# Leaving out the all-zero quarter of a causal score block, with half of the heads' keys exchanged between partition halves

## Chip, cores and metric

One core of a Trainium2 chip. The metric is the device time of one execution in microseconds (us), the lower the better. Before the change it was 703.62 us, the median of 3 runs (702.62 to 704.25).

## The reference, cut to what matters

A retention layer (attention with a decay instead of a softmax) followed by a dense layer with a gated activation. Batch 4, 8 heads, 768 positions, head size 64; then 3072 tokens through 512 -> 2048 -> 512.

```python
def _attn_ref(q, k, v):
    ...
    for t in range(S):
        state = gamma[None, :, None, None] * state + np.einsum('bhd,bhe->bhde', k[:, :, t], v[:, :, t])
        y[:, :, t] = scale * np.einsum('bhd,bhde->bhe', q[:, :, t], state)
    return y

def _moe_ref(x, w_in, w_out):
    h = x @ w_in
    g = h * (1.0 / (1.0 + np.exp(-1.702 * h)))
    return g @ w_out
```

## The kernel before

All is fp32. The sequence is cut into 24 chunks of 128 positions. For a chunk the kernel computes the scores of its 128 queries against its own 128 keys, multiplies them with a mask that holds the decay and is zero where the key is later than the query, and takes the values with them; what lies before the chunk comes from a state of 64x64 per head. Chunks are woven into the dense layer's matmuls. From chunk 8 on (block 2 of four chunks) they are "late": they run between the down-projections, in a steady pattern.

The heads lie as pairs (r, s): r is the head's half of the partitions in the transposed q and k, s its place there. `i` below is r and `h` is the half of the keys.

```python
    def attend(j, f=None):          # scores of chunk j, and the rest of chunk f = j - 1
        if j is not None:
            p = ps_a.tile([P, 2, HP, P], F32, name="pa", tag="pa")
            kt, qt = KT.pop(j), QT[j]
            for hp in range(HP):
                for h in range(2):
                    for i in range(2):
                        r, t = slice(i * D, (i + 1) * D), slice(h * D, (h + 1) * D)
                        pe.matmul(p[t, i, hp, :], kt[r, hp, t], qt[r, hp, :], start=True, stop=True)
        if f is not None:
            finish(f)
        if j is not None:
            AT[j] = home(j, "at")
            for i in range(2):
                dve.tensor_mul(AT[j][:, i], p[:, i], mask[:, i])
            if j > 2 * CB:
                decay(j)            # GpSimd: keys times their decay, for the state
        ...

    def finish(j):
        ...
        if c:                       # what the state gives: 64 rows x 64 columns of the array
            for out, s, r in where:
                k = slice(r * D, (r + 1) * D)
                pe.matmul(out, old[k, s, :], qt[k, s, :], start=(s < 2), stop=False, ...)
        for out, s, r in where:     # values: 128 rows x 64 columns
            pe.matmul(out, vn[:, HP * r + s, :], a[:, r, s, :], ...)
        if c < NC - 1:              # update of the state: 128 rows x 64 columns, 64 moving columns
            ...
```

At the end of a block GpSimd also makes four sums of X, the input of the next block's up-projection (`sums_x`), which TensorE needs in its third group of products.

Of the kernel before, what the change touches and what calls it, by code (L numbers as in the profile page):

```python
# [9 lines left out]
F32 = mybir.dt.float32  # L10
U32 = mybir.dt.uint32
AF = mybir.ActivationFunctionType
ALU = mybir.AluOpType
P = 128
# [14 lines left out]
def kernel(  # L29
# [29 lines left out]
    pe, act, dve, pool, sp = nc.tensor, nc.scalar, nc.vector, nc.gpsimd, nc.sync  # L59
    ctx.enter_context(tc.manual_schedule(engines={mybir.EngineType.PE}))  # L60

    B, H, S, D = q.shape
    NT, DM = out.shape
    DFF = moe_w_in.shape[1]
    HP = H // 2
    NC = S // P
    NCH = B * NC
    CB = 4
# [9 lines left out]
    const = ctx.enter_context(tc.tile_pool(name="const", bufs=1))  # L78
    one = ctx.enter_context(tc.tile_pool(name="one", bufs=1))
    two = ctx.enter_context(tc.tile_pool(name="two", bufs=2))  # L80
    ps_a = ctx.enter_context(tc.tile_pool(name="ps_a", bufs=1, space=bass.MemoryType.PSUM))
# [13 lines left out]
    X1 = W2[:, 6].rearrange("p (s c) t -> p s c t", s=4)  # L95
    rowd = const.tile([P, HP, P], F32, name="rowd")
    cold = const.tile([P, 2 * H], F32, name="cold")
    whole = const.tile([P, 2, 2], F32, name="whole")
    ident = const.tile([P, P], F32, name="ident")
    mask = const.tile([P, 2, HP, P], F32, name="mask")  # L100
    state = [const.tile([P, HP, D], F32, name=f"state{i}") for i in range(2)]


    QKV = {}

    def load(j, what="qkv"):


        b, c = divmod(j, NC)
        rows = slice(c * P, (c + 1) * P)  # L110

        def plain(name, src, tag, bufs, pairs=False, engine=sp):
            t = two.tile([P, H, D], F32, name=name + "_in", tag=tag, bufs=bufs)
            QKV[name, j] = t
            src = src[b, :, rows, :].rearrange("h p d -> p h d")
            if pairs:
                for i in range(2):
                    engine.dma_start(t[:, i:H:2, :], src[:, i * HP:(i + 1) * HP, :])
            else:
                sp.dma_start(t, src)  # L120

        if j < 2 * CB:
            if "q" in what:
                plain("q", q, "q_sq", 2, True)
                plain("kn", k, "k_sq", 2, True, sp if j else act)
        elif "q" in what:
            for name, src in (("q", q), ("k", k)):
                t = two.tile([P, HP, P // C4, C4], F32, name=name + "_sq")
                for r0 in range(0, P, C4):
                    d0 = r0 % D  # L130
                    for hp in range(HP):
                        tc.keep_in_program_order(sp.dma_start(
                            t[r0:r0 + C4, hp],
                            src[b, hp + HP * (r0 // D), rows, d0:d0 + C4].rearrange("(s p) d -> p s d", p=C4)))
                QKV[name, j] = t
        if "v" in what:
            if j >= 2 * CB and c < NC - 1:
                plain("kn", k, "kn", 1)
            plain("v", v, "v", 2)
# [63 lines left out]
    QT, KT, KD, AT = {}, {}, {}, {}  # L203

    def home(j, name):

        at = ["qT", "kT", "kd", "at"].index(name)
        shape = [[HP, P], [HP, P], [H, D], [2, HP, P]][at]
        if j >= 2 * CB:
            return one.tile([P] + shape, F32, name=name, tag=name, bufs=2 - (at > 0))  # L210
        if at < 3:
            t = G[:, at, j % 2 * 2:j % 2 * 2 + 2]
            return t.rearrange("p s t -> p (s t)").rearrange("p (a b) -> p a b", a=shape[0])
        return G[:, 3 + j % 2].rearrange("p s t -> p (s t)").rearrange("p (a b c) -> p a b c", a=2, b=HP)
# [22 lines left out]
    def decay(j):  # L237

        if j % NC == NC - 1:
            return  # L240
        KD[j] = home(j, "kd")
        x = QKV.pop(("kn", j)).rearrange("p h d -> p (h d)")
        x = x.rearrange("p (s r d) -> p r s d", s=HP, r=2) if j < 2 * CB else x.rearrange("p (r s d) -> p r s d", r=2, s=HP)
        pool.tensor_mul(KD[j].rearrange("p (r s) d -> p r s d", r=2), x,  # L244
                        cold[:, H:2 * H].rearrange("p (r s) -> p r s", r=2)[:, :, :, None].to_broadcast([P, 2, HP, D]))

    def attend(j, f=None):


        if j is not None:  # L250
            p = ps_a.tile([P, 2, HP, P], F32, name="pa", tag="pa")
            kt, qt = KT.pop(j), QT[j]
            for hp in range(HP):
                for h in range(2):
                    for i in range(2):
                        r, t = slice(i * D, (i + 1) * D), slice(h * D, (h + 1) * D)
                        pe.matmul(p[t, i, hp, :], kt[r, hp, t], qt[r, hp, :], start=True, stop=True)  # L257
        if f is not None:
            finish(f)
        if j is not None:  # L260
            AT[j] = home(j, "at")
            for i in range(2):
                dve.tensor_mul(AT[j][:, i], p[:, i], mask[:, i])  # L263
            if j > 2 * CB:
                decay(j)
        if f is not None and f + 2 < 2 * CB:
            load(f + 2, "v")
        if j is not None and 2 * CB < j < NCH - 1:
            load(j + 1, "v")

    def finish(j):
        c = j % NC
        old, new = state[c % 2], state[(c + 1) % 2]
        vn, a, qt = QKV.pop(("v", j)), AT.pop(j), QT.pop(j)


        y = ps_a.tile([P, 2, HP, P], F32, name="py", tag="py")
        where = [(y[s % 2 * D:(s % 2 + 1) * D, r, s // 2, :], s, r) for s in range(HP) for r in range(2)]
        if c:
            for out, s, r in where:  # L280
                k = slice(r * D, (r + 1) * D)
                pe.matmul(out, old[k, s, :], qt[k, s, :], start=(s < 2), stop=False, skip_group_check=True)  # L282
        for out, s, r in where:
            pe.matmul(out, vn[:, HP * r + s, :], a[:, r, s, :], start=(not c and s < 2), stop=(s >= 2),  # L284
                      skip_group_check=True)
        if c < NC - 1:

            kd = KD.pop(j)
            u = y[:, 0, 2:4, :].rearrange("p o t -> p (o t)").rearrange("p (s d) -> p s d", s=HP)
            for s in range(HP):  # L290
                for r in range(2):
                    pe.matmul(u[r * D:(r + 1) * D, s, :], kd[:, HP * r + s, :], vn[:, HP * r + s, :],  # L292
                              start=False, stop=True, skip_group_check=True)
        half, t0 = divmod(j % CB * P, TH)
        x = X1 if j // CB == 1 else X
        dve.tensor_mul(x[:, 2 * half:2 * half + 2, :, t0:t0 + P], y[:, :, 0:2, :],
                       rowd.rearrange("p (r o) t -> p r o t", r=2))
        if c == 0:
            dve.tensor_copy(new, u)
        elif c < NC - 1:  # L300
            pool.tensor_mul(new, old, whole.rearrange("p a b -> p (a b)")[:, :, None].to_broadcast([P, HP, D]))
            dve.tensor_add(new, new, u)
# [168 lines left out]
    first = const.tile([P, 1], F32, name="first")  # L471
# [10 lines left out]
            pe.transpose(idle[:, 0, :], ident, ident)  # L482


    for i in range(2):
        for hp in range(HP):
            h = HP * i + hp
            dve.tensor_copy(mask[:, i, hp, :], cold[:, h:h + 1].to_broadcast([P, P]))
    m3 = mask.rearrange("s i h t -> s (i h) t")
    pool.affine_select(out=m3, in_=m3, compare_op=ALU.is_ge, fill=0.0, base=0,  # L490
                       pattern=[[0, H], [1, P]], channel_multiplier=-1)

    def chunks(first, last):

# [30 lines left out]
    between = chunks(CB + 1, 2 * CB - 1) + [lambda: attend(None, 2 * CB - 1)]  # L525
    for n, unit in enumerate([(1, p) for p in range(3)] + [(half, p) for p in range(3, NP) for half in range(2)]):
        up0(*unit, "xxyx"[n % 4])
        if n % 2 == 0:
            narrow()
        if n in (0, 2, 4, 6, 8, 9, 11):  # L530
            between.pop(0)()
    for f in range(NFF):
        up1(f)
        if f % 2 == 0:
            narrow()
        if f >= NFF - 4:
            sums_w2(2 * (f - NFF + 4))
        if f >= NFF - 2:
            load(2 * CB + f - NFF + 2, "qkv" if f == NFF - 2 else "qk")
    for m in range(NB):  # L540
        between = []
        if m == 0:
            between = [lambda: turn(2 * CB), lambda: attend(2 * CB), lambda: None, lambda: None, lambda: turn(2 * CB + 1)]
        elif m == 1:
            between = [lambda: (decay(2 * CB), load(2 * CB + 1, "v"))] + chunks(2 * CB + 1, 3 * CB)[1:]
        elif 1 < m < NB - 2:
            between = chunks((m + 1) * CB + 1, (m + 2) * CB)
        elif m == NB - 2:
            between = chunks((m + 1) * CB + 1, NCH - 1) + [lambda: attend(None, NCH - 1)]
# [59 lines left out]
```

## Time and profile before

| | before |
|---|---|
| time, median of 3 | 703.62 us |
| TensorE busy | 686.3 of 701.9 us |
| one late chunk, from its first record to the next full-array matmul | 3.01 us |
| of it scores / state / values / update | 0.93 / 0.54 / 0.93 / 0.61 us |
| first down-projection to the end of the program | 539.0 us |

A record is one matmul instruction in the trace. The rows of the chunk are read from start to start in TensorE's timeline, because the records' lengths overlap. The prediction below shows those lines.

### The profile page before, as it was taken

The numbers are of one execution on the slowest core, as the hardware profiler recorded it, in microseconds if no ns is written. First come the engines' busy times: TensorE is split into PE (matmuls) and PEld (weight loads), VectorE is DVE, ScalarE is ACT, GpSimd is POOL, SyncE is SP. The second block draws the span as 40 slices with busy tenths as digits, with TensorE's granted clock in tenths as the row PEclk, the third lists the DMA queues.
The fourth block names the chain that finished last, engine by engine and source line by source line (L and its number), as shares of the span: only waits on it lengthen the run. The fifth ranks groups of instructions, "written<-read, shape, count | busy, mean of one in ns | idle before, by whom it ended". The sixth has DMA issues, their size and how long they took to land.

```text
span 701.9 us, 11046 instructions
## 1 busy us (share of the span) xinstructions
PE 686.3 (98%) x4493; PEld 572.5 (82%) x4493; DVE 361.5 (52%) x521; ACT 125.8 (18%) x197; POOL 129.7 (18%) x126
## 2 busy tenths in 40 slices
PE   6799999999999999999999999999999999999997
PEld 5588885447888888888888888888888888888886
DVE  3989889993711822443742453453345362344241
ACT  3213333311000001331000332000333000233000
POOL 4221000000466404000324000132200143000030
PEclk9899999999999999999999999999999999999999
DMA  9884343421130224200334300324300210000001
GB/s 230 264 231 133 135 136 135 138 35 28 28 65 27 63 46 103 46 1 15 72 62 91 65 1 8 72 45 90 74 0 3 60 30 13 34 1 1 15 1 45
DMA packets 138754, 46.36 MB, mean 66 GB/s; under 512 B 130176, under 2 KB 131216, under 8 KB 138704
## 3 DMA queue, kind: packets, MB, share of 16 engines
q1 hardware_dynamic: 134704, 38.84, 23.2%
q0 software_dynamic: 1856, 5.52, 2.1%
q10 hardware_dynamic: 2144, 1.31, 0.6%
q8 instruction: 35, 0.57, 0.3%
q14 instruction: 15, 0.12, 0.1%
HBM read 39.33 MB, written 6.29 MB: 65 GB/s over the span
## 4 chain that ended last, share of the span: by engine, by line
PE 93%; DVE 5%; DMA 1%; ACT 0%; SPq 0%; issue 0%; ACTq 0%
PE pd L432 39%; PE px L381 16%; PE py L381 12%; PE ph L329 8%; PE ph L342 8%; PE py L284 4%; PE pa L257 3%; PE py L292 1%; PE py L282 1%; DMA q_in<-in_q_dram 1%; DVE W L371 1%; DVE G L371 1%; PE pt L225 1%; DVE G L372 1%; DVE W L372 1%; DVE W L198 0%
## 5 line engine op out<-in xcount | busy, mean ns | idle before, releaser
L432 PE MATMUL pd<-W,G 128*128 128x256 f32 x1120 | 247.4, 381 | 0.4 <-DVE G L372 0.3
L432 PEld LDWEIGHTS pd<-W,G 128*128 128x128 f32 x1120 | 211.4, 190 | 30.4 <-DVE G L372 1.2
L381 PE MATMUL px<-X,W 128*128 128x256 f32 x512 | 119.0, 379 | 0.0
L381 PEld LDWEIGHTS px<-X,W 128*128 128x128 f32 x512 | 97.3, 190 | 13.2
L381 PE MATMUL py<-X,W 128*128 128x256 f32 x384 | 90.7, 379 | 0.0
L381 PEld LDWEIGHTS py<-X,W 128*128 128x128 f32 x384 | 73.0, 190 | 9.9
L263 DVE TENSOR_TENSOR at<-pa,mask 128x512 f32<-128x512 f32 x32 | 21.7, 686 | 79.6 <-PE py L284 70.8
L329 PE MATMUL ph<-X,W 128*128 128x256 f32 x256 | 60.9, 397 | 1.6 <-DVE W L198 0.9
L329 PEld LDWEIGHTS ph<-X,W 128*128 128x128 f32 x256 | 49.9, 199 | 9.7 <-DVE W L198 1.3
L342 PE MATMUL ph<-W,W 128*128 128x512 f32 x128 | 55.1, 592 | 0.0
L244 POOL TENSOR_TENSOR kd<-kn_in,cold 128x512 f32<-128x512 f32 x13 | 13.5, 1038 | 208.9 <-PE py L292 179.4
L342 PEld LDWEIGHTS ph<-W,W 128*128 128x128 f32 x128 | 24.3, 190 | 30.2 <-issue 29.2
L373 POOL TENSOR_TENSOR G<-G 128x512 f32<-128x512 f32 x20 | 29.5, 1480 | 95.0 <-DVE G L372 92.2
L310 DVE TENSOR_TENSOR G<-G,sg 128x512 f32<-128x512 f32 x48 | 33.0, 688 | 13.7 <-ACT sg L308 13.7
L308 ACT ACTIVATE sg<-G 128x512 f32<-128x512 f32 x48 | 30.2, 630 | 51.0 <-DVE G L391 30.7
L424 POOL DMA_DIRECT2D out_dram<-o x20 | 14.9, 744 | 128.5 <-DVE o L423 128.5
L308 ACT ACTIVATE sg<-ph 128x512 f32<-128x512 f32 x32 | 19.1, 597 | 100.6 <-PE ph L329 49.8
L432 PE MATMUL pd<-W,W 128*128 128x256 f32 x160 | 35.8, 381 | 0.4 <-DVE W L372 0.3
L432 PEld LDWEIGHTS pd<-W,W 128*128 128x128 f32 x160 | 30.2, 190 | 5.7 <-DVE W L372 1.2
L391 DVE TENSOR_TENSOR G<-py,p 128x512 f32<-128x512 f32 x16 | 11.1, 691 | 37.8 <-PE py L381 37.8
L419 ACT ACTIVATE u<-pd 128x512 f32<-128x512 f32 x6 | 3.6, 597 | 148.5 <-PE pd L432 148.5
L423 DVE TENSOR_TENSOR o<-pd,vv 128x512 f32<-128x512 f32 x12 | 7.7, 686 | 35.6 <-ACT vv L419 35.6
(102 smaller groups left out, 655.9 us busy)
## 6 DMA issues: line engine op xcount, KB each, us to landing
v_in<-in_v_dram SPq DMA_DIRECT2D x24, 256.0 KB, 3.5
W<-in_moe_w_in_dram SPq DMA_DIRECT2D x12, 512.0 KB, 4.8
W<-in_moe_w_out_dram SPq DMA_DIRECT2D x10, 512.0 KB, 3.7
out_dram<-o POOLq DMA_DIRECT2D x20, 256.0 KB, 2.7
q_sq<-in_q_dram SPq DMA_DIRECT2D x256, 16.0 KB, 1.7
k_sq<-in_k_dram SPq DMA_DIRECT2D x256, 16.0 KB, 1.7
kn_in<-in_k_dram SPq DMA_DIRECT2D x13, 256.0 KB, 3.2
G<-in_moe_w_out_dram SPq DMA_DIRECT2D x6, 512.0 KB, 3.7
```

The costliest lines, as they stand in the source:

```text
L257: pe.matmul(p[t, i, hp, :], kt[r, hp, t], qt[r, hp, :], start=True, stop=True)
L263: dve.tensor_mul(AT[j][:, i], p[:, i], mask[:, i])
L284: pe.matmul(out, vn[:, HP * r + s, :], a[:, r, s, :], start=(not c and s < 2), stop=(s >= 2), skip_group_check=True)
L308: act.activation(s, h, AF.Sigmoid, scale=1.702)
L310: dve.tensor_mul(g, h[:, i], s[:, i])
L329: pe.matmul(h[:, ab], w, X[:, 2 * half + c // 2, c % 2, :], start=(ab == 0 and c == 0), stop=(c == 3), skip_group_check=True)
L342: pe.matmul(h, w, X1[:, c // 2:4:2, c % 2, :], start=(c == 0), stop=(c == 3))
L371: dve.tensor_sub(a[2], a[0], a[2])
L373: pool.tensor_sub(a[1], a[1], a[0])
L381: pe.matmul(acc[:, u, :], W1[:, 2 * d + u, sa, c, :], X[:, sb, c, :], start=(start and u == 0 and c == 0), stop=(stop and c == 1), skip_gr ...
L424: (pool if m < NB - 1 else act).dma_start(rows[th, e], o)
L432: pe.matmul(p0[:, n, :], g1(m, p, sa)[:, n * P:(n + 1) * P], W2[:, sb, p, :], start=(new and p == 0 and n == 0), stop=(last and p == NP - ...
```

## The change

A block of 128 queries by 128 keys under a causal mask has one quarter that is zero throughout: the first 64 queries against the last 64 keys. The change neither computes that quarter of the scores nor lets all of it into the value products. Scores are computed in quarters of the array, and the output's column half is the half of the keys. So that the short products do not all lie on one column half, heads 2 to 5 get the halves of their keys exchanged on the partitions. k and v of late chunks are then loaded in four pieces, and these heads have their own decays and mask.

```diff
+    def moved(r, s):
+        return r ^ s // 2
 ...
-            if pairs:
+            if late(j):
+                for i in range(2):
+                    sp.dma_start(t[:, 6 * i:6 * i + 2, :], src[:, 6 * i:6 * i + 2, :])
+                    sp.dma_start(t[i * D:(i + 1) * D, 2:6, :], src[(1 - i) * D:(2 - i) * D, 2:6, :])
+            elif pairs:
 ...
+    def scores(j):
 ...
+        def product(r, s, h, t0):
+            c, k = (h ^ moved(r, s) if late(j) else h) * D, slice(r * D, (r + 1) * D)
+            pe.matmul(p[c:c + D, r, s, t0:], kt[k, s, h * D:(h + 1) * D], qt[k, s, t0:], start=True, stop=True)
+        if late(j):
+            for s in range(2):
+                for r, o, h in ((0, 0, 0), (0, 0, 1), (1, 0, 1), (1, 0, 0), (0, 2, 0), (1, 2, 0), (0, 2, 1), (1, 2, 1)):
+                    product(r, s + o, h, h * D)
 ...
+        if late(j):     # decayed: three multiplications, the zero quarter of `at` stays as it was cleared
+            dve.tensor_mul(a[:, :, :, D:], p[:, :, :, D:], mask[:, :, :, D:])
+            ...
+            dve.tensor_mul(a2, x2, m2)
+            dve.tensor_mul(a[D:, 2:6, :D], x[D:, 2:6, :D], m[D:, 2:6, :D])
 ...
+        if late(j):     # finish, after the state's products
+            for s, r in heads[:HP]:
+                k = slice(r * D, (r + 1) * D)
+                add(r, s, vn[k, HP * r + s, :], a[k, r, s, :D], slice(0, D))
+            between()   # the next chunk's scores
+        for s, r in heads:
+            t = slice(D if late(j) and s < 2 else 0, P)
+            add(r, s, vn[:, HP * r + s, :], a[:, r, s, t], t)
 ...
+    tc.keep_in_program_order(pool.memset(at2, 0.0))
+    for h in range(2):
+        for i in range(2):
+            for to, src, c in (...):
+                tc.keep_in_program_order(pool.dma_start(cold2[to, c], col_decay[src, c]))
+    make_mask(range(2, 6), cold2, [(slice(0, D), D), (slice(D, P), 0)])
```

More of the change, by code (lines that the diff above doesn't have):

```diff
@@ L97 @@
     cold = const.tile([P, 2 * H], F32, name="cold")
+    cold2 = const.tile([P, 2 * H], F32, name="cold2")
+    at2 = const.tile([P, 2, HP, P], F32, name="at2")
     whole = const.tile([P, 2, 2], F32, name="whole")
@@ L104, with late @@
     QKV = {}
+    def late(j):
+        return j >= 2 * CB
+    def moved(r, s):
+        return r ^ s // 2
     def load(j, what="qkv"):
@@ L209, in home @@
         if j >= 2 * CB:
-            return one.tile([P] + shape, F32, name=name, tag=name, bufs=2 - (at > 0))
+            return at2 if at == 3 else one.tile([P] + shape, F32, name=name, tag=name, bufs=2 - (at > 0))
         if at < 3:
@@ L244, in decay @@
         pool.tensor_mul(KD[j].rearrange("p (r s) d -> p r s d", r=2), x,
-                        cold[:, H:2 * H].rearrange("p (r s) -> p r s", r=2)[:, :, :, None].to_broadcast([P, 2, HP, D]))
-    def attend(j, f=None):
-        if j is not None:
-            p = ps_a.tile([P, 2, HP, P], F32, name="pa", tag="pa")
-            kt, qt = KT.pop(j), QT[j]
-            for hp in range(HP):
-                for h in range(2):
-                    for i in range(2):
-                        r, t = slice(i * D, (i + 1) * D), slice(h * D, (h + 1) * D)
-                        pe.matmul(p[t, i, hp, :], kt[r, hp, t], qt[r, hp, :], start=True, stop=True)
-        if f is not None:
-            finish(f)
-        if j is not None:
-            AT[j] = home(j, "at")
-            for i in range(2):
-                dve.tensor_mul(AT[j][:, i], p[:, i], mask[:, i])
+                        (cold2 if late(j) else cold)[:, H:2 * H].rearrange("p (r s) -> p r s", r=2)[:, :, :, None].to_broadcast([P, 2, HP, D]))
@@ new lines, in scores @@
+    def scores(j):
+        p = ps_a.tile([P, 2, HP, P], F32, name="pa", tag="pa")
+        kt, qt = KT.pop(j), QT[j]
+        def product(r, s, h, t0):
[5 more added lines that the diff above has]
+                    product(r, s + o, h, h * D)
+        else:
+            for s in range(HP):
+                for h in range(2):
+                    for r in range(2):
+                        product(r, s, h, 0)
+        return p
@@ new lines, in decayed @@
+    def decayed(j, p):
+        a = AT[j] = home(j, "at")
+        if late(j):
+            dve.tensor_mul(a[:, :, :, D:], p[:, :, :, D:], mask[:, :, :, D:])
+            a, x, m = [t.rearrange("p r s t -> p (r s) t") for t in (a, p, mask)]
+            a2, x2, m2 = [t[:D].rearrange("p (g e) t -> p g e t", g=4)[:, 0:4:3, :, :D] for t in (a, x, m)]
+            dve.tensor_mul(a2, x2, m2)
+            dve.tensor_mul(a[D:, 2:6, :D], x[D:, 2:6, :D], m[D:, 2:6, :D])
+        else:
+            for i in range(2):
+                dve.tensor_mul(a[:, i], p[:, i], mask[:, i])
@@ L264, in attend @@
+    def attend(j, f=None):
+        p = []
+        if f is not None:
+            finish(f, lambda: j is not None and p.append(scores(j)))
+        else:
+            p.append(scores(j))
+        if j is not None:
+            decayed(j, p[0])
             if j > 2 * CB:
@@ L269, in attend, with finish @@
             load(j + 1, "v")
-    def finish(j):
+    def finish(j, between):
         c = j % NC
@@ L277, in finish, with add @@
         y = ps_a.tile([P, 2, HP, P], F32, name="py", tag="py")
-        where = [(y[s % 2 * D:(s % 2 + 1) * D, r, s // 2, :], s, r) for s in range(HP) for r in range(2)]
+        heads = [(s, r) for s in range(HP) for r in range(2)]
+        started = set()
+        def add(r, s, v, x, t):
+            first = (r, s % 2) not in started
+            started.add((r, s % 2))
+            pe.matmul(y[s % 2 * D:(s % 2 + 1) * D, r, s // 2, t], v, x, start=first, stop=False, skip_group_check=True)
+        if not late(j):
+            between()
         if c:
-            for out, s, r in where:
+            for s, r in heads:
                 k = slice(r * D, (r + 1) * D)
-                pe.matmul(out, old[k, s, :], qt[k, s, :], start=(s < 2), stop=False, skip_group_check=True)
-        for out, s, r in where:
-            pe.matmul(out, vn[:, HP * r + s, :], a[:, r, s, :], start=(not c and s < 2), stop=(s >= 2),
-                      skip_group_check=True)
+                add(r, s, old[k, s, :], qt[k, s, :], slice(0, P))
+        if late(j):
+            for s, r in heads[:HP]:
+                k = slice(r * D, (r + 1) * D)
+                add(r, s, vn[k, HP * r + s, :], a[k, r, s, :D], slice(0, D))
+            between()
+        for s, r in heads:
+            t = slice(D if late(j) and s < 2 else 0, P)
+            add(r, s, vn[:, HP * r + s, :], a[:, r, s, t], t)
         if c < NC - 1:
@@ L289, in finish @@
             u = y[:, 0, 2:4, :].rearrange("p o t -> p (o t)").rearrange("p (s d) -> p s d", s=HP)
-            for s in range(HP):
-                for r in range(2):
-                    pe.matmul(u[r * D:(r + 1) * D, s, :], kd[:, HP * r + s, :], vn[:, HP * r + s, :],
-                              start=False, stop=True, skip_group_check=True)
+            for s, r in heads:
+                pe.matmul(u[r * D:(r + 1) * D, s, :], kd[:, HP * r + s, :], vn[:, HP * r + s, :],
+                          start=False, stop=True, skip_group_check=True)
         half, t0 = divmod(j % CB * P, TH)
@@ L482, in keep_warm, with make_mask @@
             pe.transpose(idle[:, 0, :], ident, ident)
-    for i in range(2):
-        for hp in range(HP):
-            h = HP * i + hp
-            dve.tensor_copy(mask[:, i, hp, :], cold[:, h:h + 1].to_broadcast([P, P]))
     m3 = mask.rearrange("s i h t -> s (i h) t")
-    pool.affine_select(out=m3, in_=m3, compare_op=ALU.is_ge, fill=0.0, base=0,
-                       pattern=[[0, H], [1, P]], channel_multiplier=-1)
+    def make_mask(heads, decays, keys):
+        for h in heads:
+            dve.tensor_copy(m3[:, h, :], decays[:, h:h + 1].to_broadcast([P, P]))
+        part = m3[:, heads[0]:heads[-1] + 1, :]
+        for k, first in keys:
+            pool.affine_select(out=part[k], in_=part[k], compare_op=ALU.is_ge, fill=0.0, base=-first,
+                               pattern=[[0, len(heads)], [1, P]], channel_multiplier=-1)
+    make_mask(range(H), cold, [(slice(0, P), 0)])
     def chunks(first, last):
@@ L531 @@
             between.pop(0)()
+    tc.keep_in_program_order(pool.memset(at2, 0.0))
+    for h in range(2):
+        for i in range(2):
+            for to, src, c in ((slice(0, P), slice(0, P), slice(h * H + 6 * i, h * H + 6 * i + 2)),
+                               (slice(i * D, (i + 1) * D), slice((1 - i) * D, (2 - i) * D), slice(h * H + 2, h * H + 6))):
+                tc.keep_in_program_order(pool.dma_start(cold2[to, c], col_decay[src, c]))
+    make_mask(range(2, 6), cold2, [(slice(0, D), D), (slice(D, P), 0)])
     for f in range(NFF):
```

## The prediction

> **What bounds the kernel now.** I read the page first: its busy times, its slices and its chain.
>
> ```profile
> span 701.9 us, 11046 instructions
> PE 686.3 (98%) x4493; PEld 572.5 (82%) x4493; DVE 361.5 (52%) x521; ACT 125.8 (18%) x197; POOL 129.7 (18%) x126
> PE   6799999999999999999999999999999999999997
> PE 93%; DVE 5%; DMA 1%; ACT 0%; SPq 0%; issue 0%; ACTq 0%
> ```
>
> TensorE (PE) is busy 98% of the span, from the third slice on without a visible gap, and the chain that ended last runs through it for 93%. So a nanosecond taken out of TensorE's stream after the first 35 us is a nanosecond off the end, unless a new wait takes its place; time on DVE, POOL or the queues is free as long as TensorE is not made to wait.
>
> Then the timeline of TensorE in one stretch of block 2's chunks, which shows what one chunk costs (start, length, instruction, count):
>
> ```profile
> 250.88 1.10 PE L257 MATMUL pa<-qT,kT 64*64 64x128 f32 x32
> 251.81 0.62 PE L282 MATMUL py<-qT,state 64*64 64x128 f32 x16
> 252.35 1.15 PE L284 MATMUL py<-at,v_in 128*64 128x128 f32 x16
> 253.28 0.69 PE L292 MATMUL py<-v_in,kd 128*64 128x64 f32 x16
> 253.89 10.63 PE L432 MATMUL pd<-W,G 128*128 128x256 f32 x48
> ```
>
> A chunk takes 253.89 - 250.88 = 3.01 us: scores 0.93 us, state product 0.54, values 0.93, state update 0.61. Each fp32 product of the program is two records (16 score products, x32), and their lengths overlap, so I count from start to start.
>
> The single records of the same stretch show how they are paced. Scores and state products (64 rows by 64 columns of the array) start in groups of four, 6 to 7 ns apart, one for each quarter of the array, and the next group follows 109 ns later. Values (128 rows by 64 columns) run on two column halves, each with its own cadence of 109 ns. State updates, 64 moving columns instead of 128, have a cadence of 57.5 ns. So a **step** of a quarter or half costs 109 ns at 128 moving columns and 57.5 ns at 64: time goes with the columns, and nearly nothing is fixed. The quarters also do not wait for each other in program order. In the values the program has four records for one half, then four for the other, and both start within 15 ns. That is what decides whether mixed lengths pack.
>
> The check of this reading: scores are 8 steps of 109 = 872 ns plus 52 ns for the first weight load (first step 161 instead of 109), 924 against 925 measured. State is 4 x 109 = 436, then 109 until the first value record. Values are 872 + 52 and a hiccup of 44 ns in the second half. Updates are 8 x 57.5 = 460. With a skew of 15 ns and 93 ns to the next full-array matmul that adds to 3.01 us.
>
> **What the Trainium skill says.** "TensorEngine Tiling (Array Packing)", section "Key Properties", says that tiles operate independently and can load weights and multiply in parallel, while a change of tiling mode drains the engine. The trace agrees: four quarters 7 ns apart, and at the change from quarters to halves 109 ns plus 52 ns of exposed weight load. "TensorE: Matmul & The Clock Gate", section "What overlaps and what doesn't", says matmuls are "strict FIFO, no reordering". Read strictly, a short product behind a long one would gain nothing; the trace of the values (two halves together, where program order has four records of one half first) differs, and I go by the trace. The same page, "Back-to-back issue gap", gives about N/2.4 + 2.5 ns per pass warm; twice that for N=64 would be 58 ns and for N=128 112 ns, an estimate that the records' 57.5 and 109 bear out. "PSUM — Partial Sum Buffer", section "PSUM bank collisions raise a hardware error", says that different row tiles cannot access one bank at the same time. No run so far shows it, but it explains the new order: row half r always writes bank r.
>
> **The change part by part.** It holds for chunks 8 to 23, 16 of the 24.
>
> Scores: 16 products stay 16, but the eight for the second half of the keys take only the second 64 queries. If the keys were not exchanged, the short ones would all lie on the same column half; with the exchange each quarter gets, per chunk, 4 long and 4 short records. Steps: 4 x 109 + 4 x 57.5 = 666 ns instead of 872. **Minus 206 ns a chunk.**
>
> Values: for heads with s below 2 (four heads, r either) the first 64 queries need only the first 64 keys. Four new products of 64 rows and 64 moving columns run on the four quarters at once: 2 steps x 57.5 = 115 ns. The same heads' full products shrink from 128 to 64 moving columns: per half 4 x 57.5 + 4 x 109 = 666 instead of 872. **Minus 206 plus 115 = minus 91 ns a chunk.** I leave the 44 ns hiccup as it is. The new products lie between state and scores, all in quarters, so the changes of mode stay three per chunk (full, quarters, halves, full) and their cost stays.
>
> Sum: 297 ns x 16 = 4.75 us: 3.30 from the scores, 1.46 from the values.
>
> DVE: two multiplications at 128x512 (684 ns each) become one of 128x512 and two of 64x256. A 128x256 TENSOR_TENSOR takes 0.41 us in the groups by form, so 684 + 2 x 410 = 1.50 us for 1.37, plus 0.13 us a chunk, 2 us in all on an engine 52% busy: no cost at the end. What follows from them is needed only a chunk later, over 10 us.
>
> Loads: keys and values of a late chunk come in four pieces instead of one (kn x13 becomes 52, v x16 becomes 64), the same bytes in the same 256-byte rows. SyncE takes about 0.4 to 0.5 us to issue one, so about 3 us more a chunk on a queue that already needs 15 to 18 us for the 32 pieces of q and k, where chunks in a burst are 13.6 us apart. I went through the margins: the tightest are the transposes at 475.6 us, whose k had landed at 472.4, and at 258.3, landed 253.7. In both, most of the added pieces come behind the loads that matter, or in front of a point where the queue waits for DVE anyway; I get 0 to 1.5 us of delay against 3.2 to 6 us of margin. Hidden.
>
> Setup: POOL gets one memset (128x1024, about 1.1 us as the mask's select of that size), eight small DMAs (0.6 to 0.7 us each as L504), and two selects; DVE gets four copies (221 ns each as L488). It falls after the first part of the dense layer, about 108 us, where POOL is idle from 108.5 to 179.
>
> ```profile
> 107.91 0.61 POOL L301 TENSOR_TENSOR state<-state,whole 128x256 f32<-128x256 f32 x1 [8.90 <-DVE state L302]
> 179.12 0.77 POOL L424 DMA_DIRECT2D out_dram<-o  x1 [70.60 <-DVE o L423]
> 105.00:122.00 17.00, 17.00 (x48) 8.79 (x47) 15.65 (x22) 5.72 (x8) 0.61 (x1) 1.00 0.41 140
> 122.00:140.00 18.00, 18.00 (x43) 7.99 (x42) 17.73 (x22) 5.94 (x9) 0.00 (x0) 1.00 0.43 133
> 140.00:158.00 18.00, 18.00 (x43) 7.98 (x42) 17.86 (x26) 3.61 (x6) 0.00 (x0) 1.00 0.22 35
> ```
>
> The windows (length, PE, PEld, DVE, ACT, POOL busy) show what matters there: TensorE never waits, but DVE is full, 17.86 of 18 us. A DVE stuck behind these small loads moves everything after it. It is ahead of TensorE by some 8 us: its last sums of the second weights end at 158.5 us and are first read about 166.4. I expect a stall of at most a few us, so nothing at the end; for the tail of this I add 0.3 us.
>
> 703.62 - 4.75 + 0.3 = 699.2 us.
>
> **Rivals.** (1) *Mixed lengths do not pack.* If a short record holds its place until the long ones of its group end, scores stay at 872 ns, the full value products probably at 872 too, and the new ones are pure cost: 115 x 16 = 1.8 us more, 705.5 us. For it speaks the skill's sentence on order; against it, that the halves run out of program order in the values, and single updates follow as soon as their own half is free. There is one sign of limited lookahead, the 44 ns hiccup where the program changes halves. A mild form, one such hiccup more per phase (three x 45 ns x 16 = 2.2 us), gives 701. (2) *Setup blocks DVE.* If the copies go to the head of DVE's queue before the eight DMAs are issued (108.5 + 1.1 + 4 x 0.65, and some 2.7 us to land, the page's median for a POOL store, so 115), DVE stands for up to 6 to 8 us, which eats the 8 us lead: 0 to 2 us at the end, 699 to 701. (3) *Loads come late.* With 3 us more issue time per chunk a transpose could wait and DVE with it; TensorE would stall by the part beyond the margin, in one or two chunks: at most 2 us. (4) *More than I count:* with shorter value products the hiccup may vanish, 44 x 16 = 0.7 us: 698.2.
>
> **Range and chances.** Packing as computed I hold at some 65%, a partial loss at 25%, none at 10%. The three runs of before spread over 1.6 us. That makes 697.7 to 702.8. The threshold of 2% is 14 us; all of the late chunks' scores and values together take 16 x 1.85 = 30 us, of which a sixth can go, so faster by 2% is out of reach, and slower would need a stall that no margin above suggests. Faster 0.01, same 0.985, slower 0.005.
>
> **What would show it.** In the changed profile TensorE has 8 records a chunk more, 4493 + 128 = 4621, and stays at 98%. A late chunk goes from 3.01 to about 2.71 us from its first record to the next full-array one, with scores at about 0.67 us, the four new products at 0.12, and values at 0.77. If scores stay near 0.87, rival 1 holds. If TensorE's wait for DVE between 105 and 185 us grows beyond the 0.4 us it has now, it is rival 2; if DVE's transposes wait for q or k by over 1 us, rival 3. I am wrong if the late chunks shrink by less than 0.2 us each, or if they shrink as computed and the time does not.

## The result and the profile after

The changed kernel takes 699.87 us (median of 4, 698.71 to 700.41), before 703.86 in the same rounds. The ratio is 0.9941, 95% interval 0.9925 to 0.9957. Ratios here are the mean time of one kernel's fast runs over that of the other's of the same rounds, so not quite the ratio of the medians quoted.

The page of the changed kernel: TensorE has 4621 records (4493 + 128) and is as full as before.

```profile
span 698.6 us, 11471 instructions
PE 681.8 (98%) x4621; PEld 569.2 (81%) x4621; DVE 365.5 (52%) x541; ACT 125.9 (18%) x197; POOL 137.6 (20%) x137
PE   6699999999999999999999999999999999999997
```

TensorE's timeline of the chunk that answers to the one in the prediction (start, length, instruction, count):

```profile
251.97 0.67 PE L328 MATMUL py<-qT,state 64*64 64x128 f32 x16
252.45 0.29 PE L328 MATMUL py<-at,v_in 64*64 64x64 f32 x8
252.57 0.85 PE L269 MATMUL pa<-qT,kT 64*64 64x128 f32 x32
253.35 0.94 PE L328 MATMUL py<-at,v_in 128*64 128x64 f32 x16
254.07 0.68 PE L351 MATMUL py<-v_in,kd 128*64 128x64 f32 x16
254.68 10.63 PE L491 MATMUL pd<-W,G 128*128 128x256 f32 x48
```

254.68 - 251.97 = 2.71 us instead of 3.01. The four new value products take 0.12 us. Scores take 0.78 us up to the first value record, which includes the 0.11 us of the change from quarters to halves, so 0.67. A merged line names the shape of its first record only; half of the 32 score records have 64 columns.

Adding up the stretches of attention in each trace, and the stretch from the first record of the first down-projection to the end of the program, gives this table for all runs. "Start" is where the last part before that stretch begins (first 512-column record of the dense layer).

| run | late chunk with all parts | attention from chunk 8 on | first down-projection to end | start | time (median) |
|---|---|---|---|---|---|
| before | 3.010 | 46.05 | 539.04 | 107.88 | 703.62 |
| after | 2.714 | 41.32 | 533.93 | 109.66 | 699.87 |
| after_again | 2.714 | 41.33 | 533.93 | 109.86 | 699.63 |
| e1_scores_only | 2.803 | 42.75 | 535.36 | 107.52 | 699.84 |
| e2_values_only | 2.920 | 44.62 | 538.77 | 107.61 | 703.18 |
| e3_no_exchange | 2.996 | 45.87 | 538.85 | 109.20 | 704.12 |
| e4_by_quarter | 3.762 | 58.09 | 550.70 | 108.02 | 715.44 (1 run) |
| e5_alternate | 2.667 | 40.56 | 533.16 | 109.07 | 698.12 |
| e8_pool_order | 2.714 | 41.32 | 558.02 | 108.49 | 723.25 (1 run) |
| e9_pieces_only | 3.010 | 46.05 | 538.61 | 109.08 | 704.42 (1 run) |

After against before: attention gives 46.05 - 41.32 = 4.73 us. The whole stretch gives 5.11; the other 0.38 lies behind the last matmul (4.58 us from the start of TensorE's last record to the end before, 4.19 after). That tail goes with the loads in four pieces: it is 4.14 to 4.20 in the eight traces that have them, e9_pieces_only with the old matmuls among them, and 4.57 and 4.58 in the two that have not (e3_no_exchange and before). So it belongs to the change, though not to its matmuls. In the records of SyncE the program's end has a row of eight semaphore instructions in the kernel before where the changed one has a single one; why the loads change that is not shown.

### The profile page after: what moved, and what is told of

Read it like the earlier page. It is cut to its first block, busy times and chain, and to the rows that moved or that the text cites. A ratio compares the mean times of both kernels' runs of the same rounds, so it can differ in the third digit from the quotient of the medians.

```text
span 698.6 us, 11471 instructions
## 1 busy us (share of the span) xinstructions
PE 681.8 (98%) x4621; PEld 569.2 (81%) x4621; DVE 365.5 (52%) x541; ACT 125.9 (18%) x197; POOL 137.6 (20%) x137
## 4 chain that ended last, share of the span: by engine, by line
PE 88%; DVE 8%; DMA 1%; ACT 1%; SPq 1%; issue 1%; POOL 1%; ACTq 0%; DVEq 0%; POOLq 0%
PE pd L491 39%; PE px L440 16%; PE py L440 12%; PE ph L401 8%; PE ph L388 5%; PE py L328 5%; PE pa L269 2%; PE py L351 1%; DMA kn_in<-in_k_dram 1%; DVE W L210 1%; ACT W L204 1%; DVE G L430 1%; DVE W L430 1%; DVE W L214 1%; DVE G L295 1%
## 5 line engine op out<-in xcount | busy, mean ns | idle before, releaser
L388 PE MATMUL ph<-X,W 128*128 128x256 f32 x256 | 59.3, 389 | 1.6 <-DVE W L214 0.9
L288 DVE TENSOR_TENSOR at<-pa,mask 128x512 f32<-128x512 f32 x16 | 11.0, 689 | 74.1 <-PE py L328 65.4
```

Of the source, the lines that this page charges most:

```text
L388: pe.matmul(h[:, ab], w, X[:, 2 * half + c // 2, c % 2, :], start=(ab == 0 and c == 0), stop=(c == 3), skip_group_check=True)
```

## The experiments

All eight gave the reference's result. Numbers of the parts that a verdict rests on are in the table above.

### The scores alone

```diff
-            for s, r in heads[:HP]:                                  # no products of 64 rows
-                k = slice(r * D, (r + 1) * D)
-                add(r, s, vn[k, HP * r + s, :], a[k, r, s, :D], slice(0, D))
             between()
         for s, r in heads:
-            t = slice(D if late(j) and s < 2 else 0, P)
+            t = slice(0, P)
```

> The scores' part of the change alone: scores short and keys exchanged as after the change, but the values are multiplied whole again (8 products of 128 rows and 128 queries, no products of 64 rows). My theory (every quarter or half of the array runs its own stream, 109 ns a record of 128 columns and 57.5 of 64): a late chunk of 2.72 us becomes 2.72 + 0.091 = 2.81 us, the time 699.9 + 16 x 0.091 = 701.3 us; scores stay at 0.67 us plus the change of mode. Rival, that the four new value products bring nothing or cost as much as they save: 2.72 us and 699.9 us, same as the changed kernel.

The chunk took 2.803 us, 0.089 more than with both parts, and the stretch to the end 535.36, which is 1.43 more than 533.93 (1.46 expected). The time by itself could not show it: 699.84 us, ratio 0.9951 (0.9931 to 0.9971), against 0.9941 for the whole change. In the profiles the start alone differs by 2.1 us (107.52 against 109.66), more than the effect. So the value products do bring 89 ns of the 91 expected, and it takes the trace to see it.

### The values alone

```diff
-                    product(r, s + o, h, h * D)
+                    product(r, s + o, h, 0)
-            dve.tensor_mul(a[:, :, :, D:], p[:, :, :, D:], mask[:, :, :, D:])   # and the two that follow
+            for i in range(2):
+                dve.tensor_mul(a[:, i], p[:, i], mask[:, i])
```

> The values' part alone: keys exchanged, scores and masks whole (16 products of 128 queries, two multiplications of 128x512), values split as after the change. My theory: a late chunk takes 2.72 + 0.206 = 2.93 us and the time is 699.9 + 16 x 0.206 = 703.2 us. Both parts add up, so e1 and e2 together give back the whole gain of the late chunks (0.29 us each). If the parts share a cost (a change of mode, a hiccup), their sum would differ from 0.29 us by more than 0.03.

The chunk took 2.920 us, 0.206 more than with both parts: as computed, and 0.089 + 0.206 = 0.295 is the whole gain of a chunk. But the stretch to the end was 538.77, only 0.27 less than before, though attention was 1.43 shorter. The waits of TensorE name one that neither the kernel before nor the changed one has, in this kernel's timelines of TensorE and of POOL (in brackets: idle before, and what ended it):

```profile
278.29 1.99 PE L437 MATMUL px<-X,W 128*128 128x256 f32 x8 [1.30 <-POOL X L412]
```

```profile
269.04 1.26 POOL L411 TENSOR_TENSOR X<-X 128x512 f32<-128x512 f32 x1
275.97 1.04 POOL L260 TENSOR_TENSOR kd<-kn_in,cold 128x512 f32<-128x512 f32 x1 [5.68 <-DMA kn_in<-in_k_dram]
276.97 1.26 POOL L412 TENSOR_TENSOR X<-X 128x512 f32<-128x512 f32 x1
```

The scheduler put the decay of the next chunk's keys between the second and the third sum of X. The decay waited 5.68 us for keys that arrive in pieces, the third sum stood behind it in GpSimd's queue, and TensorE waited 1.30 us for that sum. With the two slow steps around it (1.68 and 0.32 us from record to record instead of 0.22 each) the wait cost some 1.6 us, and that is what is missing: 539.04 - 1.43 for attention - 0.39 for the shorter tail is 537.22. So the time, 703.18 us where 703.2 was expected, agrees by luck: the expectation had no such wait in it. With the changed kernel's own order the wait did not happen:

```profile
270.99 1.27 POOL L415 TENSOR_TENSOR X<-X 128x512 f32<-128x512 f32 x1
272.33 1.27 POOL L416 TENSOR_TENSOR X<-X 128x512 f32<-128x512 f32 x1
277.30 1.04 POOL L260 TENSOR_TENSOR kd<-kn_in,cold 128x512 f32<-128x512 f32 x1 [3.70 <-DMA kn_in<-in_k_dram]
```

Two more runs below follow this up.

### Short scores without the exchange

```diff
     def moved(r, s):
-        return r ^ s // 2
+        return 0
```
with loads, decays and mask as before, and values whole as in the first experiment.

> Scores short, but without the exchange of keys on the partitions (loads and decays as in the kernel before, values whole, because without the exchange the short value products would put two row halves on one bank). Then all short products lie on one column half. My theory: the other half still has 8 records of 109 ns, so scores stay at 0.87 us, a late chunk at about 3.01 us, and the time is that of the kernel before within 0.1%, 703.9 us. Rival, that what counts is the number of columns streamed in all, wherever they go: scores 0.67 us, chunk 2.81 us, 701.3 us like e1.

The stretch to the end was 538.85, before 539.04; the chunk 2.996, before 3.010; the ratio 1.0003 (0.9975 to 1.0031). This kernel's chunk, scores and what follows them:

```profile
239.11 1.04 PE L264 MATMUL pa<-qT,kT 64*64 64x128 f32 x32
240.08 1.15 PE L321 MATMUL py<-at,v_in 128*64 128x128 f32 x16
```

Scores to values is 0.97 us, 0.86 without the change of mode, though a quarter of the columns is gone. With the exchange it is 0.78 us:

```profile
237.08 0.85 PE L269 MATMUL pa<-qT,kT 64*64 64x128 f32 x32
237.86 1.14 PE L328 MATMUL py<-at,v_in 128*64 128x128 f32 x16
```

(The second fence is the first experiment's, which has the same short scores and whole values.) So in these two runs, with as many columns in all, it is the fullest quarter that counts, and the gain from the scores hangs on the exchange.

### One quarter of the array after the other

```diff
-            for s in range(2):
-                for r, o, h in ((0, 0, 0), (0, 0, 1), (1, 0, 1), (1, 0, 0), (0, 2, 0), (1, 2, 0), (0, 2, 1), (1, 2, 1)):
-                    product(r, s + o, h, h * D)
+            for r, c in ((0, 0), (0, 1), (1, 0), (1, 1)):
+                for s in range(HP):
+                    h = c ^ moved(r, s)
+                    product(r, s, h, h * D)
```

> The changed kernel with the same 16 score products in another program order: all of one quarter of the array, then all of the next. It tells how far ahead of program order a quarter can start. Strict program order: 4 x 0.67 = 2.7 us of scores a chunk, 732 us in all. A window so deep that all 32 records fit: 0.67 us, no change, 700 us. My reading of the 44 ns hiccup, that each quarter holds about four records and what follows in program order waits until the quarter before has room: second quarter starts at 0.44 us, third at 0.67, fourth at 0.90, end at 1.56 us, so plus 0.9 us a chunk and about 714 us.

It took 715.44 us. The same products in this order took 1.83 us up to the values, 1.72 without the change of mode:

```profile
239.65 1.90 PE L269 MATMUL pa<-qT,kT 64*64 64x128 f32 x32
241.48 0.94 PE L329 MATMUL py<-at,v_in 128*64 128x64 f32 x16
```

In the single records the second quarter starts 0.445 us after the first, when the first quarter's fifth record starts (0.44 expected). Neither strict program order (2.7 us) nor a window for all 32 records (0.67) fits. A quarter runs ahead of program order by about four records of another, as far as the second quarter's start shows it; the end at 1.72 instead of 1.56 us shows that my sum is rough for the later quarters.

### Values alternately from both halves

```diff
-        for s, r in heads:
+        for s, r in [(o + i, r) for o in (0, 2) for r in range(2) for i in range(2)]:
             t = slice(D if late(j) and s < 2 else 0, P)
```

> The changed kernel with the whole value products taken alternately from the two column halves (0, 1, 0, 1) instead of two of one half and two of the other. Theory, that the 44 ns hiccup comes from a half that cannot start records further ahead in program order than the other half's few places allow: the hiccup goes, a late chunk takes 2.67 instead of 2.714 us, the stretch from the first down-projection to the end 533.2 instead of 533.9 us, and the time falls by 0.7 to 1.0 us (early chunks have it too) to about 699.0. Rival, that it comes from something that order doesn't touch (a bank, the switch from 64 to 128 columns): no change.

The chunk took 2.667 us and the stretch 533.16, 0.77 less than after: the hiccup is gone, and the two halves now run 6 to 8 ns apart throughout. The time is 698.12 us, ratio 0.9922 (0.9901 to 0.9943), beside after_again with 0.9943 on the same chip. It is the fastest version found; its lead over the changed kernel is shown by the trace, the intervals of the two ratios overlap. Its chunk:

```profile
251.78 0.85 PE L269 MATMUL pa<-qT,kT 64*64 64x128 f32 x32
252.56 0.89 PE L328 MATMUL py<-at,v_in 128*64 128x64 f32 x16
253.28 0.63 PE L351 MATMUL py<-v_in,kd 128*64 128x64 f32 x16
```

Values and updates together now end (next full-array record at 253.85) 1.29 us after the first value record, 1.33 in the changed kernel.

### The changed kernel again

No edit.

> The changed kernel again, unedited, beside the next one on the same chip. In the first profile the stretch before the second layer of block 1 (first 512-column record of the dense layer) began 1.8 us later than before (109.66 against 107.88 us), and the three experiments with the same setup had it at 107.5 to 108.0. Theory, that this is the start's own spread: it lies anywhere between 107 and 110 us now, while the stretch from the first down-projection to the end is 533.9 within 0.4 us as in the first profile. Rival, that the setup costs 1.8 us: 109.5 us or more again.

The stretch was 533.93 again. The start came at 109.86 us, so this run alone spoke for the rival. Over all traces it does not hold: kernels with the whole setup have 109.66, 109.86, 107.52, 107.61, 108.02, 109.07 and 108.49 (mean 108.6), those without its mask and loads 107.88, 109.20 and 109.08 (mean 108.7). The traces also tell where the spread lies and what the setup does cost. A multiplication on DVE ahead of the setup (`W<-py,rowd`, L355 in the changed kernel) starts at 83.93 us before, 85.40 after and 85.89 in after_again, and at 83.6 to 85.9 over all ten: the spread is there already, while the setup's first instruction comes at 100.45 us. From that multiplication to "start" it is 23.95 to 23.97 us in seven traces, three without the setup and four with it, and 23.82 in e5_alternate, whose early chunks are shorter. In two it is more, 24.26 in the first profile and 24.33 in e8_pool_order: there the setup costs 0.3 to 0.4 us up to this point. What spreads the first 84 us was not looked into.

### Decay ahead of the sums on GpSimd

`tc.keep_in_program_order(...)` around the multiplication in `decay` and the four subtractions of `sums_x`, so that GpSimd takes them as the program has them.

```diff
-        pool.tensor_mul(KD[j]..., x, ...)
+        tc.keep_in_program_order(pool.tensor_mul(KD[j]..., x, ...))
-        pool.tensor_sub(X[:, 5], X[:, 3], X[:, 4])          # and the other three
+        tc.keep_in_program_order(pool.tensor_sub(X[:, 5], X[:, 3], X[:, 4]))
```

> The changed kernel with GpSimd's decay of the keys kept ahead of the sums of X that follow it in the program (in the changed kernel the scheduler has put the sums first in every block). Theory, that the loads in four pieces do come late and only this order hides it: at the end of blocks 1, 2 and 3 the third sum ends some 4, 8 and 7 us after TensorE needs it (277.95 us, 385.86 us and 493.3 us in the changed kernel), TensorE waits for POOL by about 20 us in all, time 715 to 720 us. Rival, that the later loads are hidden in any case: no wait for POOL over 0.5 us, 700 us.

723.25 us, with the attention unchanged at 41.32. TensorE's longest wait, from the table of waits (us in all, times, longest):

```profile
PE px L440 <- POOL X L415: 18.6, 3, 8.0
```

So later loads are not hidden in any case; the scheduler's order hides them. The stretch grew by 558.02 - 533.93 = 24.1 us, 5.5 more than the waits. Most of that, 4.6 us when the records are added up, is TensorE's clock: after each of the three waits its 256-column records come 427 ns apart instead of 216 for about 3 us, and the clock granted from 398.8 to 402.0 us was 0.55. "TensorE: Matmul & The Clock Gate", section "Loop structure matters more than you think", says that a long idle (8 us in its example) lets the clock drop to half; the traces agree, for waits of 4.0, 6.6 and 8.0 us here, while after the wait of 1.30 us in e2_values_only the records stayed at 216 ns:

```profile
387.14 1.89 PE L440 MATMUL px<-X,W 128*128 128x256 f32 x8
388.87 1.89 PE L440 MATMUL py<-X,W 128*128 128x256 f32 x8
398.81 3.40 PE L440 MATMUL px<-X,W 128*128 128x256 f32 x8 [8.04 <-POOL X L415]
```

### The pieces alone

The kernel before with this one edit (no exchange):

```diff
-            if pairs:
+            if j >= 2 * CB:
+                for i in range(2):
+                    sp.dma_start(t[:, 6 * i:6 * i + 2, :], src[:, 6 * i:6 * i + 2, :])
+                    sp.dma_start(t[i * D:(i + 1) * D, 2:6, :], src[i * D:(i + 1) * D, 2:6, :])
+            elif pairs:
```

> The kernel before with one thing of the change, the loads of late keys and values in four pieces (unexchanged). The scheduler puts the sums of X ahead of the decay here as in the changed kernel. Theory: the keys land 3 to 8 us later, and TensorE waits for nothing new; the stretch from the first down-projection to the end is 539.0 us within 0.4 as in the kernel before, the time 703 to 704.5 us. Rival, that the pieces cost time by themselves (queue or DVE waiting): over 540 us in that stretch.

538.61 us for the stretch, 0.43 less than the 539.04 before, which is the shorter tail spoken of above (4.14 against 4.58), and no new wait of TensorE in that stretch. In pieces the loads cost nothing by themselves, provided GpSimd's sums go first, and here they do.

## Why the prediction was right or wrong

**The step times: right.** 109 ns for 128 and 57.5 for 64 moving columns gave 2.71 us a chunk; 2.714 was measured. The scores were to give 206 ns and gave 206 (e2 against after), the values 91 and gave 89 (e1 against after). All late chunks were to give 4.75 us and gave 4.73. One sentence of the working was too strong: that the quarters do not wait for each other in program order. They run ahead of it by some four records and no further.

**Rival 1, mixed lengths do not pack: fell.** But its ground is real: program order does matter within some four records (one quarter after the other: 1 us more a chunk). The order that the change chose keeps within that. The hiccup of 44 ns that I left in the sum hangs on program order too: with alternating halves it went, 47 ns a chunk. That both come from one and the same limit is likely, but not shown.

**Rival 2, setup blocks DVE: there, and small.** It came earlier than predicted, not in the gap after 108 us: GpSimd cleared the new tile at 100.45 us and issued the small loads from 101.34 on. In the first profile DVE stood 1.70 us for the decays of the exchanged heads.

```profile
106.44 0.23 DVE L548 COPY mask<-cold 128x128 f32<-128x128 f32 x1 [1.70 <-DMA cold<-in_col_decay_dram]
```

The chain of work that ended last in this stretch (start, length, what) leads from the loads through that copy to TensorE's next part:

```profile
103.58 2.77 DMA cold<-in_col_decay_dram
106.44 0.23 DVE mask L548
109.00 0.61 DVE W L355
109.66 5.42 PE ph L401 x12
```

TensorE's first 512-column record came 0.30 us late (0.51 us after the record before it, 0.22 in the kernel before), and the next one another 0.10, which is why the part that follows took 55.04 instead of 54.93 us. That makes 0.40 us, where 0.3 was set aside. In the second profile DVE stood 0.74 us, and TensorE lost nothing.

**Rival 3, loads come late: the sum was right for a reason I had not seen.** The prediction said "Hidden" after looking at the transposes alone. Their tightest margin did hold: the transposes at 474.1 us had their k at 472.8, a margin of 1.3 us where before had 3.2. But the path with the least room was another: keys landed, decay on GpSimd, sums of X behind it in the same queue, third group of the up-projection. In the kernel before, the third sum ended at 277.27 us and TensorE used it at 277.46:

```profile
272.55 1.03 POOL L244 TENSOR_TENSOR kd<-kn_in,cold 128x512 f32<-128x512 f32 x1 [4.83 <-DMA kn_in<-in_k_dram]
276.00 1.27 POOL L356 TENSOR_TENSOR X<-X 128x512 f32<-128x512 f32 x1
277.46 1.89 PE L381 MATMUL px<-X,W 128*128 128x256 f32 x8
```

The change's pieces land up to 8 us later (the decay of block 2's end moved from 381.3 to 389.7 us; first line before, second after):

```profile
381.32 1.04 POOL L244 TENSOR_TENSOR kd<-kn_in,cold 128x512 f32<-128x512 f32 x1 [1.73 <-DMA kn_in<-in_k_dram]
389.66 1.04 POOL L260 TENSOR_TENSOR kd<-kn_in,cold 128x512 f32<-128x512 f32 x1 [7.73 <-DMA kn_in<-in_k_dram]
```

With the decay ahead of the sums that would have eaten the gain several times over: 24 us in the run that forces it, 1.6 in the run where one decay slipped in. (The forced order is harsher than the old one, which in blocks 2 and 3 had two sums ahead of the decay. With the old order and the changed kernel's landing times the third sum would end some 4, 6 and 4.5 us too late at the three block ends, about 15 us; an estimate from its timelines.) With the loads in pieces the scheduler put the decay behind the sums at all three block ends (in e2_values_only at two), in e9_pieces_only too, where this is the only edit; the two kernels without pieces have it ahead of the third sum each time. By what rule it chooses is not shown. So the predicted time was right partly because of a reordering that nobody wrote into the change: the step "Hidden" was right by luck.

The issue cost was also low in my estimate: four pieces each of k and v take SyncE 4.9 us where the two loads took 1.1 (the queue's timeline, 341.7 to 346.6 after, 340.8 to 341.9 before), so 3.8 more, not 3.

**The end result.** 699.2 was predicted, 699.87 and 699.63 measured. What remains is smaller than the spread of the first 84 us, and the runs do not say more about it. In the two profiles the span fell by 3.2 us: 1.8 later at the start (0.3 of it the setup), 0.1 more up to the first down-projection, 5.1 less from there on, 0.4 of which is the tail that the prediction did not have. So what the runs confirm of the mechanism is the 4.73 us of attention and the size of the setup's delay; how close the total came is partly chance.

## What to carry to other kernels

When small matmuls run on parts of the array at once, count the columns of each part, not their sum: here short products paid only where every part got as many of them, and program order did best where it alternated between the parts. When a load becomes slower "off the critical path", follow its consumer's in-order queue and not only the consumer: what stands behind it there may be what TensorE reads next. And where the start of a program varies by more than the effect, compare a later stretch of the trace from one fixed record to another.

## What the Trainium skill lacked or had wrong

- "TensorE: Matmul & The Clock Gate", section "The mechanism" (under "What overlaps and what doesn't"), has matmuls as strict FIFO. Between column halves or quarters of the array the runs show otherwise: products of another quarter start before earlier ones in program order, by about four records (second quarter 0.445 us after the first in e4_by_quarter, where the first quarter's last record starts at 0.610).
- The same page gives about 4 ns from tile to tile; in fp32 on four quarters the records start 6 to 7 ns apart, on two halves 12 to 15 ns where program order has two products of a half in a row, and 6 to 8 ns where they alternate.
- "TensorEngine Tiling (Array Packing)", section "Key Properties", says that a change of mode drains the engine, without a cost: from quarters to halves 90 ns more than a step, counted from the last record's start (199 ns after 128 columns in the kernel before, 148 after 64 in the changed one; 109 ns when counted from the first of the last four), and 52 ns for the first weights.
- No page gives the time of an fp32 record of a tile as such: two records a product, each 109 ns at 128 and 57.5 ns at 64 moving columns. The prediction's estimate from the gap formula, 112 and 58, was close.
